# y as one product over 128 rows, scores in one group, and v loaded without zeros, in an RWKV-7 layer with its MLP

## The chip, the cores and the metric

The kernel runs on one core of a Trainium2 chip. The metric is device time in microseconds (us), the median of several runs of the same program.

## What is computed

An RWKV-7 recurrence for 4 batches of 8 heads (768 steps, head dimension 40), whose output, with the heads side by side, is the input of an MLP with a sigmoid-approximated GELU:

```python
for t in range(S):
    y[:, :, t] = np.einsum('bhd,bhde->bhe', rt, state)
    Sa = np.einsum('bhde,bhe->bhd', state, at)
    state_decay = state * wt[:, :, None, :] - np.einsum('bhd,bhe->bhde', Sa, bt)
    state = state_decay + np.einsum('bhd,bhe->bhde', vt, kt)
...
x = np.ascontiguousarray(attn_out.transpose(0, 2, 1, 3)).reshape(B * S, H * D)   # 3072 x 320
h = x @ w_in                                                                     # 320 x 2048
g = h * (1.0 / (1.0 + np.exp(-1.702 * h)))
return (g @ w_out).astype(np.float32)                                            # 2048 x 320
```

All is float32.

## The kernel before, in words

Time is cut into 12 chunks of 64 steps and the batches into 2 pairs, which gives 24 *units* i (chunk c, pair p). A unit holds 16 heads: a batch b of the pair, and a head index split into bits e, f and u. Within a unit the recurrence is solved in matrix form, so that only the 40x40 state z goes from unit i to unit i + 2.

**The array.** Almost every product works on a quarter of the TensorE array: 64 rows by 64 columns, four such tiles in turn (`QUARTERS`). A float32 product is two MATMULs and two weight loads, so four products of a group are 16 TensorE instructions. The helper `mm` (L270) issues all of them, which is why every MATMUL has line 270 and is told apart by its tile's name.

**A unit's steps.** `load_w`, `logarithm` and `decay` (L431 to L503) load the decays w, take logarithms (ScalarE), sum them (TensorE `ps_cum`, VectorE scans) and exponentiate: FT, GT by channel, and G by time step (L498, one ACTIVATE of 320 columns on 128 partitions). `prep` (L521 to L585) scales k and b by G into `kh` and `bh` (L535, two operations of 320 columns, GpSimd or VectorE), forms the score matrices `ps_NT` and `ps_A`, `ps_Av`, and also `ps_RV` (L575), the products of r and v, masked into the tile `RV` by VectorE (L583). `solve` (L592 to L815) forms `ps_N`, then six doubling levels (`ps_level`) whose results are copied into W and E by ScalarE and VectorE; the last level leaves 40 columns in the tile `M` (L639). `ps_saT` (L721) and its copy `saT` follow. `ps_M` (L748) multiplies saT by r, and VectorE masks it into `M` (L756). `read` (L760) then forms `ps_y`, both the output and the state update in 104 columns (64 steps and 40 state columns), as a sum of two sets of products, kh with RV and bh with M. `updated` (L775) gives the raw state `zraw` that unit i + 2 reads; `read_out` and `decayed` give x, which goes through DRAM and comes back transposed as `xT` (L805 to L815).

**The tile RV.** Its 104 columns per head are 64 for the masked products r·v and 40 for v itself. v is loaded straight into place, with zeros in the other 64 columns, which the mask operation overwrites later (L441, `in_v`).

**The MLP** (`mlp`, L822). For each chunk: `ps_up` (160 products of 256 columns), GELU on ScalarE (L835) into `g`, `ps_down` (128 products of 320 columns), a copy and an add into `ob`, and a store.

**What sets the order.** Nothing runs in program order. Every step is a `Task` with a rank, the engines that it may run on with an assumed duration on each, what it reads and writes, and the number of buffers of each tile (`plan.slots`). `Plan.order` (L97) plays a list scheduler over five engines, and emits the instructions in that order; each engine runs its own list in order. The plan has a model of how fast TensorE's instructions can be fetched (`FETCH`, `BESIDE`, `BLOCK`: 256 instructions, 3,550 ns, more beside DMA traffic) and chooses between tasks by it (`ahead`, L144). MLP products have the highest ranks, so they fill what the units leave. `paced` repeats the ordering to spread the MLP over the run. PSUM is four pairs of banks, taken and given back by the plan. All DMA is issued by SyncE (SP).

**Weights.** The MLP's weights arrive as int64 words of doubles and are decoded on the chip in ten pieces (`weight`, L367), each with some seven VectorE and ScalarE operations of 1,024 columns; `W_IN` and `W_OUT` (L239) are their ranks. All of this happens in the first 160 us.

Of the kernel before, what the change touches and what calls it, by code (L numbers as in the profile page):

```python
# [49 lines left out]

class Task:
    def __init__(self, rank, engines, fn, pair, most, size):
        self.instr, self.sbuf = engines.pop("instr", 0), engines.pop("sbuf", False)
        self.rank, self.fn, self.pair, self.most, self.size = rank, fn, pair, most, size
        self.engines = engines
        self.after, self.then, self.release = set(), [], 0.0


class Plan:
# [5 lines left out]
    BLOCK, FETCH, BESIDE, AHEAD = 256, 3550.0, 0.4, 300.0  # L65
    DELAY = {"PE": 300.0, "DVE": 60.0, "ACT": 60.0, "POOL": 150.0, "SP": 800.0}

    LATENCY, RATE, SPREAD = 1200.0, 400.0, 1.3
# [28 lines left out]
    def order(self):  # L97
# [22 lines left out]
        issued, begun, shared = 0, 0.0, 0.0  # L120

        def fetch(at):
            took = self.FETCH
            for _ in range(3):
                beside = sum(max(0.0, min(y, at + took) - max(x, at)) for x, y in running[-8:])
                took = self.FETCH + self.BESIDE / self.SPREAD * beside
            return took
# [20 lines left out]
        while coming or able:  # L148
# [20 lines left out]
            if e == "PE":  # L169
                end, begun = fetched(t, now)  # L170
                issued += t.instr
# [5 lines left out]
            if e == "SP":  # L177
                wire = max(wire, end + self.LATENCY)
                running.append((wire, wire + self.SPREAD * t.size / self.RATE))
                end = wire = running[-1][1]  # L180
# [44 lines left out]
def rwkv7_gelu_quick(ctx: ExitStack, tc: tile.TileContext, time_d, v_d, w_d, wc_d, ak_d, b_d, rv_d, w_in, w_out, out):  # L225
    nc = tc.nc
# [12 lines left out]
    W_IN, W_OUT = 12, 30  # L239
# [10 lines left out]
    plan = Plan(dict(logw=3, wc=3, G=1, wch=3, wz=2, time=2, ak=2, b=2, rv=2, FT=3, GT=1, kh=2, bh=2, bz=2,  # L250
                     A=1, Av=1, RV=2, W=3, E=2, edge=1, zraw=2, zT=1, saT=1, M=2, y=1, x=1, xT=3, g=4, ob=1), 4)
# [86 lines left out]
    kh_t, bh_t = several("kh", [128, 8, 64]), several("bh", [128, 8, 64])  # L338
    for t in kh_t + bh_t:
        nc.gpsimd.memset(t[:, :, D:], 0.0)  # L340
# [5 lines left out]
    ak_t, b_t, rv_t = several("ak", [128, 2, 8, 64]), several("b", [128, 8, 64]), several("rv", [128, 2, 8, 64])  # L346
# [76 lines left out]
    time_of = lambda i: buf("time", i, [128, 3, DM])  # L423
    ak_of, b_of, rv_of = lambda i: ak_t[i % 2], lambda i: b_t[i % 2], lambda i: rv_t[i % 2]

    RV_of = lambda i: buf("RV", i, [128, 8, 104])
# [9 lines left out]
    def load(i):  # L436
        for name, of, src, n in (("ak", ak_of, ak_d, 1024), ("time", time_of, time_d, 3 * DM), ("b", b_of, b_d, 512),
                                 ("rv", rv_of, rv_d, 1024), ("RV", RV_of, v_d, 832)):
            rows = [slice(p.start, p.start + D) for p in HALF] if i >= 2 and name in ("ak", "b", "rv") else [slice(0, 128)]

            def go(t, of=of, src=src, rows=rows):  # L441
                for p in rows:
                    nc.sync.dma_start(of(i)[p], src[i, p])
            plan.add(10 * i - 4, {"SP": 350.0 * len(rows)}, go, writes=[(name, i)] + ([("v", i)] if name == "RV" else []),
                     size=sum(p.stop - p.start for p in rows) * n * 4)


    G_of = lambda i: buf("G", i, [128, 2, 160])
# [24 lines left out]
    def decay(i):  # L473
# [3 lines left out]
        def by_time(t):  # L477
            ps, lw = psum(t, "ps_cum"), logw_of(i)
            for n in (1, 0):
                for b in BITS:  # L480
                    u = b ^ n
                    mm(ps[HALF[u], b, :160], incl[HALF[b]], lw[HALF[b], n * 160:(n + 1) * 160], True)
        plan.add(R, pe((1, 160)), by_time, reads=T("log"), uses=T("logw"), room=T("G"), writes=T("cum"), pair=("cum", i))

        def exp_channel(t):
            if i >= EARLY:
# [11 lines left out]
        plan.add(R, {"ACT": 460.0}, lambda t: nc.scalar.activation(G_of(i), psum(t, "")[:, :, :160], ACT.Exp, scale=-1.0),  # L498
                 reads=T("FT"), writes=T("G", "exps"), pair=("cum", i))
# [6 lines left out]
    def by_head(t):  # L506
        return t.rearrange("t (h d) -> t h d", h=H)

# [5 lines left out]
    saT_of = lambda i: buf("saT", i, [128, 8, 64])  # L514
    M_of = lambda i: buf("M", i, [128, 8, 104])
    xT_of = lambda c: buf("xT", c, [128, 2, NK, 128])
    kh_of, bh_of = lambda i: kh_t[i % 2], lambda i: bh_t[i % 2]
# [3 lines left out]
    def prep(i):  # L521
        R = 10 * i - 6
        T = lambda *names: [(n, i) for n in names]
        G = lambda: G_of(i).rearrange("t b (h d) -> t (b h) d", d=D)
# [9 lines left out]
        for n, (name, dst) in enumerate((("kh", kh_of), ("bh", bh_of))):  # L534
            plan.add(R + 4, {"POOL": 870.0, "DVE": 490.0, "sbuf": True}, lambda t, n=n, dst=dst: of(t.engine).tensor_mul(  # L535
                dst(i)[:, :, :D], by_head(time_of(i)[:, n]), G()), reads=T("time", "exps", "G"), writes=T(name))
# [26 lines left out]
        def times_v(t):  # L563

            ps, v_b = psum(t, "ps_Av"), time_of(i)[:, 2]
            for e, f in product(BITS, BITS):
                for b, u in QUARTERS:
                    o, h = (2 * e + f) * D, head(e, f, b, u)
                    mm(ps[HALF[u], b, o:o + D], A_of(i)[HALF[b], 4 * e + 2 * u + f], v_b[HALF[b], h * D:(h + 1) * D], o == 0)
# [4 lines left out]

        def score_RV(t):  # L575

            ps, rv = psum(t, "ps_RV"), rv_of(i)
            for e, b in product(BITS, BITS):
                for f, u in QUARTERS:
                    o, j = (2 * e + b) * 64, 4 * u + 2 * e + b  # L580
                    mm(ps[HALF[u], f, o:o + 64], rv[HALF[f], 1, j], rv[HALF[f], 0, j], o == 0)
        plan.add(R + 9, pe((4, 64)), score_RV, reads=T("rv"), room=T("RV"), pair=("RV", i))
        plan.add(R + 9, dve(512), lambda t: nc.vector.tensor_tensor(  # L583
            RV_of(i)[:, :, :64].rearrange("p (e j) t -> p e j t", e=2), psum(t, "")[:, :, :256].rearrange("p e (j t) -> p e j t", t=64),
            mask(upper), ALU.mult), reads=T("v"), writes=T("RV"), pair=("RV", i))  # L585
# [6 lines left out]
    def solve(i):  # L592
# [59 lines left out]
        def level(n, b):  # L652
# [9 lines left out]
            def go(t):  # L662
# [3 lines left out]
                for j in BITS:  # L666
                    o = j * 208
# [7 lines left out]
                if early and alone:  # L675
                    view = ps[:, :, :416].rearrange("p h (j n) -> p h j n", n=208)
                    for h, q in QUARTERS:
# [9 lines left out]
                     room=T("M") if last else [("W", s + 1)] + ([] if early and n < LEVELS - 2 else [("E", es + 1)]), pair=pair)  # L687
# [10 lines left out]
            elif last:  # L698
                plan.add(key, any2(160), lambda t: signed(
                    t, M_of(i).rearrange("p (f e b) n -> p b e f n", f=2, e=2)[:, b, :, :, 64:], item(t)[:, :, :, 64:104], i >= EARLY),  # L700
                         writes=T("M"), pair=pair)
# [19 lines left out]
        def sa_turned(t):  # L721

            ps, w, E = psum(t, "ps_saT"), W_of(6 * i + 5), E_of(last_e(i))
            for u, b in product(BITS, BITS):
                for e, f in QUARTERS:
                    o = (2 * u + b) * 64
                    mm(ps[HALF[f], e, o:o + 64], w[HALF[e], u, b, f, 64:128], E[HALF[e], u, b, f, 64:], o == 0)
# [4 lines left out]
            t, saT_of(i).rearrange("p (r j) t -> p r (j t)", r=2), psum(t, "")[:, :, :256], i >= EARLY), writes=T("saT"), pair=("saT", i))  # L732

        y_of, x_of = lambda: buf("y", i, [128, 8, 64]), lambda: buf("x", i, [128, 4, 2, 64])
        if c > 0:
            def read_state(t):

                ps, rT = psum(t, "ps_rz"), rv_of(i)[:, 0]
                for u, b in product(BITS, BITS):
                    for f, e in QUARTERS:  # L740
                        o, at = (2 * u + b) * 64, (4 * e + 2 * u + b) * D
                        mm(ps[HALF[e], f, o:o + 64], zT_of(i)[HALF[f], at:at + 64], rT[HALF[f], 4 * u + 2 * e + b], o == 0)
# [5 lines left out]
        def scores(t):  # L748

            ps, rT = psum(t, "ps_M"), rv_of(i)[:, 0]  # L750
            for e, b in product(BITS, BITS):
                for f, u in QUARTERS:
                    o = (2 * e + b) * 64
                    mm(ps[HALF[u], f, o:o + 64], saT_of(i)[HALF[f], 4 * e + 2 * u + b], rT[HALF[f], 4 * u + 2 * e + b], o == 0)
        plan.add(R + 4, pe((4, 64)), scores, reads=T("saT", "rv"), room=T("M"), pair=("M", i))
        plan.add(R + 4, dve(512), lambda t: nc.vector.tensor_tensor(  # L756
            M_of(i)[:, :, :64].rearrange("p (e j) t -> p e j t", e=2), psum(t, "")[:, :, :256].rearrange("p e (j t) -> p e j t", t=64),
            mask(upper), ALU.mult), writes=T("M"), pair=("M", i))

        def read(t):  # L760

            ps = psum(t, "ps_y")
            for b, f in product(BITS, BITS):
                o = (2 * b + f) * 104
                for m, w in ((RV_of(i), kh_of(i)), (M_of(i), bh_of(i))):
                    for u, e in QUARTERS:
                        mm(ps[HALF[e], u, o:o + 104], w[HALF[u], 4 * b + 2 * f + e], m[HALF[u], 4 * f + 2 * e + b],
                           o == 0 and w is kh_t[i % 2])
        plan.add(R + 4, pe((8, 104)), read, reads=T("RV", "M", "kh", "bh") + (T("rz") if c > 0 else []), room=T("y", "zraw"),
                 pair=("y", i))  # L770
# [43 lines left out]
        plan.add(-50, {"SP": 700.0}, part_with, reads=T("x"), writes=T("xd"), size=DM * 512)  # L814
# [161 lines left out]
```

## Time and profile before

| | |
|---|---|
| Five runs | 826.61, 841.57, 825.93, 837.47, 836.05 us |
| Median | 836.05 us |
| Profiled execution | 826.61 us, of which its span is 824.7 us |
| Instructions | 51,261, of which 24,192 MATMULs and 24,192 weight loads |
| DMA | 82.60 MB, mean 100 GB/s |
| Mean granted TensorE clock | 0.971 |

PE is TensorE's matrix work, PEld its weight loads, DVE is VectorE, ACT ScalarE, POOL GpSimd, SP SyncE. The page cuts the span into 40 slices of some 20.6 us; a digit is a busy share in tenths. The chain of waits goes back from the last instruction to whatever released each step; "issue" in it is time in which an engine waited for nothing that the profile shows. A group is given as line, engine, operation, output and inputs with shapes, count, then busy us and mean ns of one, then the idle time just before them and what ended it. In the table of stretches each engine has its busy us and, in brackets, its instructions, then the granted clock, the DMA share and GB/s.

A MATMUL's recorded duration overlaps with that of the next ones: 250 ns for a ps_y MATMUL, though 64 of them take 1.43 us together. Prices of groups are therefore taken from the chain, where one group ends as the next begins.

### The profile page before, as it was taken

How to read it: one execution, taken by the hardware profiler on the slowest of the kernel's cores; microseconds unless marked ns; L12 is line 12 of the kernel's file. 1: busy time of each engine (PE TensorE's matmuls, PEld its weight loads, DVE VectorE, ACT ScalarE, POOL GpSimd, SP SyncE). 2: the span in 40 equal slices, each digit the busy share in tenths (PEclk: the TensorE clock that was granted, in tenths of full speed). 3: DMA queues.
4: the chain of work that ended last, by engine and by line, in shares of the span. 5: the costliest groups of instructions: out<-in, count | busy, mean ns of one | idle time of the engine just before them, and what ended most of it. 6: DMA issues, size and time to landing. Idle time of an engine off the chain costs nothing.

```text
span 824.7 us, 51261 instructions
## 1 busy us (share of the span) xinstructions
PE 754.5 (91%) x24192; PEld 648.0 (79%) x24192; DVE 476.8 (58%) x757; ACT 368.3 (45%) x634; POOL 148.1 (18%) x208
## 2 busy tenths in 40 slices
PE   3575899999999988999999999999999999999997
PEld 3564777798786887789777777789799888778997
DVE  7478897845655646565566556566456566455100
ACT  4554745335346336444556345345355445233110
POOL 4020304311203202211203112022113112100000
PEclk9885899999999999999999999999999999999999
DMA  9834533322423413222324325134233223110100
GB/s 340 341 116 155 178 110 103 117 81 65 120 73 94 126 51 109 86 92 82 110 71 134 90 63 150 35 103 133 57 97 113 68 65 105 49 36 29 35 10 17
DMA packets 33018, 82.60 MB, mean 100 GB/s; under 512 B 5128, under 2 KB 11272, under 8 KB 31528
## 3 DMA queue, kind: packets, MB, share of 16 engines
q1 hardware_dynamic: 32808, 79.32, 30.3%
q8 instruction: 190, 3.11, 1.6%
q14 instruction: 20, 0.16, 0.1%
HBM read 71.43 MB, written 7.86 MB: 96 GB/s over the span
## 4 chain that ended last, share of the span: by engine, by line
PE 84%; ACT 5%; DVE 4%; issue 4%; DMA 2%; SPq 1%; ACTq 0%; DVEq 0%
PE ps_up L270 24%; PE ps_down L270 24%; PE ps_level L270 18%; PE ps_y L270 5%; PE ps_N L270 2%; PE ps_NT L270 2%; PE ps_rz L270 2%; PE ps_saT L270 1%; PE ps_A L270 1%; PE ps_M L270 1%; PE ps_zT L270 1%; PE ps_Av L270 1%; PE ps_RV L270 1%; ACT g L835 1%; ACT W L714 1%
## 5 line engine op out<-in xcount | busy, mean ns | idle before, releaser
L270 PE MATMUL ps_up<-xT,w_sb 64*64 64x256 f32 x3840 | 268.1, 380 | 6.8 <-ACT g L835 3.0
L270 PE MATMUL ps_down<-w_sb,g 64*64 64x320 f32 x3072 | 245.6, 433 | 2.2 <-issue 0.8
L270 PEld LDWEIGHTS ps_up<-xT,w_sb 64*64 64x64 f32 x3840 | 159.2, 135 | 23.8 <-issue 4.5
L270 PEld LDWEIGHTS ps_level<-W,E 64*64 64x64 f32 x5888 | 150.7, 135 | 29.3 <-ACT g L835 3.6
L714 ACT COPY W<-ps_level 128x672 f32<-128x672 f32 (+1 forms) x154 | 95.1, 620 | 170.8 <-PE ps_level L270 160.1
L270 PEld LDWEIGHTS ps_down<-w_sb,g 64*64 64x64 f32 x3072 | 134.2, 134 | 36.7 <-issue 3.9
L270 PE MATMUL ps_level<-W,E 64*64 64x64 f32 (+2 forms) x5888 | 148.1, 230 | 6.4 <-DVE E L704 1.7
L709 DVE TENSOR_TENSOR E<-twice,ps_level 128x512 f32<-128x512 f32 x120 | 81.4, 683 | 66.2 <-ACT W L714 55.8
L535 POOL TENSOR_TENSOR kh<-time,G 128x320 f32<-128x320 f32 x22 | 19.7, 893 | 450.5 <-issue 217.9
L270 PEld LDWEIGHTS ps_level<-W 64*64 64x64 f32 x2560 | 68.8, 142 | 20.7 <-issue 12.1
L270 PE MATMUL ps_level<-W 64*64 64x64 f32 (+2 forms) x2560 | 71.0, 244 | 13.4 <-issue 9.2
L835 ACT ACTIVATE g<-ps_up 128x1024 f32<-128x1024 f32 x48 | 49.1, 1023 | 54.6 <-PE ps_up L270 54.2
L799 POOL TENSOR_TENSOR x<-y,FT 128x128 f32<-128x128 f32 x84 | 46.5, 583 | 19.8 <-ACT y L791 19.6
L693 DVE TENSOR_TENSOR W<-edge,ps_level 128x672 f32<-128x672 f32 x40 | 34.0, 850 | 21.0 <-PE ps_level L270 20.3
L861 DVE TENSOR_TENSOR ob<-ob,ps_down 128x320 f32<-128x320 f32 x24 | 11.6, 484 | 58.9 <-ACT ob L859 58.4
L270 PE MATMUL ps_y<-RV,kh 64*64 64x104 f32 x768 | 37.3, 260 | 7.7 <-DVE M L756 7.6
L714 DVE COPY W<-ps_level 128x672 f32<-128x672 f32 (+1 forms) x46 | 34.4, 751 | 8.2 <-PE ps_level L270 8.1
L270 PEld LDWEIGHTS ps_y<-RV,kh 64*64 64x64 f32 x768 | 30.1, 140 | 10.6 <-DVE M L756 8.1
L270 PE MATMUL ps_y<-M,bh 64*64 64x104 f32 x768 | 37.4, 260 | 0.9 <-issue 0.9
L527 POOL TENSOR_TENSOR ak<-ak,FT 128x512 f32<-128x512 f32 x21 | 28.1, 1339 | 28.6 <-DMA ak<-in_ak 17.9
L756 DVE TENSOR_TENSOR M<-ps_M,upper 128x512 f32<-128x512 f32 x24 | 16.5, 688 | 26.3 <-PE ps_M L270 26.2
L859 ACT COPY ob<-ps_down 128x320 f32<-128x320 f32 x24 | 10.2, 426 | 47.0 <-PE ps_down L270 46.8
(111 smaller groups left out, 1015.6 us busy)
## 6 DMA issues: line engine op xcount, KB each, us to landing
time<-in_time SPq DMA_DIRECT2D x24, 480.0 KB
RV<-in_v SPq DMA_DIRECT2D x24, 416.0 KB
xT<-x_dram SPq DMA_DIRECT2D x48, 160.0 KB
ak<-in_ak SPq DMA_DIRECT2D x44, 160.0 KB
rv<-in_rv SPq DMA_DIRECT2D x44, 160.0 KB
wc<-in_wc SPq DMA_DIRECT2D x24, 264.0 KB
extra<-in_w_out SPq DMA_DIRECT2D x4, 1024.0 KB
logw<-in_w SPq DMA_DIRECT2D x24, 160.0 KB
```

Of the source, the lines that this page charges most:

```text
L270: nc.tensor.matmul(o, lhsT, rhs, start=start, stop=True, skip_group_check=True)
L527: plan.add(R, {"DVE": 690.0, "POOL": 1270.0, "sbuf": True}, lambda t: of(t.engine).tensor_mul(ahT(), ahT(), FT_of(i)), reads=T("ak", "FT") ...
L535: plan.add(R + 4, {"POOL": 870.0, "DVE": 490.0, "sbuf": True}, lambda t, n=n, dst=dst: of(t.engine).tensor_mul(dst(i)[:, :, :D], by_head(t ...
L693: plan.add(key, dve(672), lambda t: nc.vector.tensor_sub(W_of(s + 1)[:, :, b], edge[:, :, b], item(t)[:, :, :, :168]), reads=T("edge"), wr ...
L709: plan.add(key, dve(512), lambda t: nc.vector.tensor_sub(E_of(es + 1)[:, :, b].rearrange("p h j (n t) -> p h (j n) t", n=2), wide(twice).t ...
L714: plan.add(key, any2(4 * (168 - lo)), lambda t: copy(t.engine)(W_of(s + 1)[:, :, b, :, lo:], item(t)[:, :, :, lo:168]), writes=keeps, pair ...
L756: plan.add(R + 4, dve(512), lambda t: nc.vector.tensor_tensor(M_of(i)[:, :, :64].rearrange("p (e j) t -> p e j t", e=2), psum(t, "")[:, :, ...
L799: of(t.engine).tensor_mul(x[:, b ^ u, b], y_of()[:, at], FT_of(i)[:, at])
L835: plan.add(-45, act(1024), lambda t: nc.scalar.activation(g_of(c * NQ + q).rearrange("p m r n -> p r m n"), psum(t, "").rearrange("p r (m ...
L859: plan.add(-45, any2(320), lambda t: copy(t.engine)(ob_of(serial), psum(t, "")[:, 0, :DM]), writes=[("ob", serial)], pair=("down", serial))
L861: plan.add(-45, dve(320), lambda t: nc.vector.tensor_add(ob_of(serial), ob_of(serial), psum(t, "")[:, 1, :DM]), reads=[("ob", serial)], wr ...
```

## The change

- **y.** kh and bh become one tile `kb`, of 128 partitions: kh (64 steps) above bh (64 steps), for all 16 heads side by side. RV and M become one tile `RM` of 128 partitions: the masked r·v (and v) above, the masked saT·r (and the last level's result) below. y is one product over 128 rows for each of the 16 heads, instead of two over 64. `kb` is made by one operation of 640 columns instead of two of 320.
- **RM's layout** is [13, 16, 8]: 104 columns of a head are 13 runs of 8, each 16 x 8 elements from the next. The product's moving operand, the masks' output and the last level's copies use it.
- **Scores.** `ps_RV` with its own mask is gone. `scores` forms r·v and r·saT in one group of 32 products, v and saT side by side in the tile `rv`, and two mask operations write all of RM's scores. saT now lies in `rv`.
- **G** is needed in both halves of the partitions, for all 320 channels: one ACTIVATE on 128 partitions with 320 columns becomes four on 64 partitions with 320 columns each.
- **The last level** is copied to partitions 64 to 127 of RM, in two operations per batch b instead of one.
- **v** is loaded as 64 partitions of 640 contiguous elements (160 KB) instead of 128 of 832 (416 KB).
- **The plan's numbers**: `BESIDE` and the DMA model, a price `SWITCH` for a task whose number of rows differs from the last one's, SP's delay 800 to 1,300, `W_OUT` 30 to 35, buffers (xT 3 to 2, saT 1 to 2).

```diff
-    BLOCK, FETCH, BESIDE, AHEAD = 256, 3550.0, 0.4, 300.0
-    DELAY = {"PE": 300.0, "DVE": 60.0, "ACT": 60.0, "POOL": 150.0, "SP": 800.0}
+    BLOCK, FETCH, BESIDE, AHEAD = 256, 3550.0, 0.37, 300.0
+    SWITCH = 105.0
+    DELAY = {"PE": 300.0, "DVE": 60.0, "ACT": 60.0, "POOL": 150.0, "SP": 1300.0}
...
-                end, begun = fetched(t, now)
+                end, begun = fetched(t, now + (self.SWITCH if t.rows != rows else 0.0))
+                rows = t.rows
...
-    W_IN, W_OUT = 12, 30
+    W_IN, W_OUT = 12, 35
...
-                     A=1, Av=1, RV=2, W=3, E=2, edge=1, zraw=2, zT=1, saT=1, M=2, y=1, x=1, xT=3, g=4, ob=1), 4)
+                     A=1, Av=1, RM=2, W=3, E=2, edge=1, zraw=2, zT=1, saT=2, y=1, x=1, xT=2, g=4, ob=1), 4)
...
-                for p in rows:
-                    nc.sync.dma_start(of(i)[p], src[i, p])
+                if name == "RM":
+                    nc.sync.dma_start(of(i)[HALF[0], 8:].rearrange("p g j n -> p (g j n)"), src[i])
+                    return
+                for p in rows:
+                    nc.sync.dma_start(of(i)[p, :2] if name == "rv" else of(i)[p], src[i, p])
...
-        plan.add(R, {"ACT": 460.0}, lambda t: nc.scalar.activation(G_of(i), psum(t, "")[:, :, :160], ACT.Exp, scale=-1.0),
+        def exp_time(t):
+            for h in BITS:
+                for p in HALF:
+                    nc.scalar.activation(G_of(i)[p, :, h * 160:(h + 1) * 160], psum(t, "")[HALF[h], :, :160], ACT.Exp, scale=-1.0)
+        plan.add(R, {"ACT": 1800.0}, exp_time, reads=T("FT"), writes=T("G", "exps"), pair=("cum", i))
...
-        for n, (name, dst) in enumerate((("kh", kh_of), ("bh", bh_of))):
-            plan.add(R + 4, {"POOL": 870.0, "DVE": 490.0, "sbuf": True}, lambda t, n=n, dst=dst: of(t.engine).tensor_mul(
-                dst(i)[:, :, :D], by_head(time_of(i)[:, n]), G()), reads=T("time", "exps", "G"), writes=T(name))
+        plan.add(R + 4, {"POOL": 1700.0, "DVE": 830.0, "sbuf": True}, lambda t: of(t.engine).tensor_mul(
+            kb_of(i)[:, :, :D], time_of(i)[:, :2 * DM].rearrange("t (h d) -> t h d", d=D),
+            G_of(i).rearrange("t b (h d) -> t (b h) d", d=D)), reads=T("time", "exps", "G"), writes=T("kb"))
...
-        def score_RV(t):
-            ps, rv = psum(t, "ps_RV"), rv_of(i)
-            for e, b in product(BITS, BITS):
-                for f, u in QUARTERS:
-                    o, j = (2 * e + b) * 64, 4 * u + 2 * e + b
-                    mm(ps[HALF[u], f, o:o + 64], rv[HALF[f], 1, j], rv[HALF[f], 0, j], o == 0)
...
-                plan.add(key, any2(160), lambda t: signed(
-                    t, M_of(i).rearrange("p (f e b) n -> p b e f n", f=2, e=2)[:, b, :, :, 64:], item(t)[:, :, :, 64:104], i >= EARLY),
-                         writes=T("M"), pair=pair)
+                for u in BITS:
+                    plan.add(key, any2(160), lambda t, u=u: signed(
+                        t, RM_of(i)[HALF[1], 8:, 8 * b + 4 * u:8 * b + 4 * u + 4].rearrange("p g j n -> p j g n"),
...
         def scores(t):
-            for e, b in product(BITS, BITS):
-                for f, u in QUARTERS:
-                    o = (2 * e + b) * 64
-                    mm(ps[HALF[u], f, o:o + 64], saT_of(i)[HALF[f], 4 * e + 2 * u + b], rT[HALF[f], 4 * u + 2 * e + b], o == 0)
+            for j, (b, u, e) in enumerate(product(BITS, BITS, BITS)):
+                for f, h in QUARTERS:
+                    mm(ps[HALF[h], f, j * 64:(j + 1) * 64], rv[HALF[f], 1 + h, 4 * e + 2 * b + u],
+                       rv[HALF[f], 0, 4 * e + 2 * b + u], j == 0)
+        plan.add(R + 4, pe((8, 64)), scores, reads=T("saT", "rv"), room=T("RM"), pair=("M", i))
+        for f in BITS:
+            plan.add(R + 4, dve(512), lambda t, f=f: nc.vector.tensor_tensor(
+                RM_of(i)[:, :8].rearrange("p g (j f) n -> p f j g n", f=2)[:, f],
...
         def read(t):
-            for b, f in product(BITS, BITS):
+            for b, f, u, e in product(BITS, BITS, BITS, BITS):
                 o = (2 * b + f) * 104
-                for m, w in ((RV_of(i), kh_of(i)), (M_of(i), bh_of(i))):
-                    for u, e in QUARTERS:
-                        mm(ps[HALF[e], u, o:o + 104], w[HALF[u], 4 * b + 2 * f + e], m[HALF[u], 4 * f + 2 * e + b],
-                           o == 0 and w is kh_t[i % 2])
+                mm(ps[HALF[e], u, o:o + 104].rearrange("p (g n) -> p g n", n=8), kb_of(i)[:, 8 * b + head(e, f, b, u)],
+                   RM_of(i)[:, :, 8 * b + 4 * u + 2 * e + f], o == 0)
+        plan.add(R + 4, {"PE": 1375.0, "instr": 64, "rows": 128}, read, reads=T("RM", "kb") + (T("rz") if c > 0 else []),
+                 room=T("y", "zraw"), pair=("y", i))
```

## The prediction

> **What bounds the kernel now.** I read the page first, then the table of stretches, then the chain of waits in order of time, then the groups.
>
> ```profile
> PE 754.5 (91%) x24192; PEld 648.0 (79%) x24192; DVE 476.8 (58%) x757; ACT 368.3 (45%) x634; POOL 148.1 (18%) x208
> PE   3575899999999988999999999999999999999997
> PEclk9885899999999999999999999999999999999999
> DMA  9834533322423413222324325134233223110100
> q8 instruction: 190, 3.11, 1.6%
> PE 84%; ACT 5%; DVE 4%; issue 4%; DMA 2%; SPq 1%; ACTq 0%; DVEq 0%
> ```
>
> The array (PE) is busy in nine tenths of every slice after the first seven, and 84% of the chain is PE. To see whether busy means working, I priced the groups from the chain, where they follow each other: 64 ps_y MATMULs take 1.43 us, 16 of ps_up 0.865, 16 of ps_down 1.08, 32 with 64 columns (ps_M, ps_A and their like) 0.46, 32 of ps_N 0.72, 8 of ps_cum 0.27; ps_level averages 17.4 ns each. By the counts: ps_up 208 us, ps_down 207, ps_level 152, the eight 64-column groups 87, ps_y 34, ps_N 17, ps_cum 6.5: **712 us of array work** in a span of 824.7. So 113 us are lost. Where?
>
> ```profile
> 0.00:50.00 50.00, 26.03 (x987) 23.81 (x987) 32.27 (x57) 23.10 (x43) 9.77 (x27) 0.90 0.84 315
> 50.00:100.00 50.00, 33.77 (x1085) 30.40 (x1089) 39.96 (x49) 30.10 (x50) 11.76 (x14) 0.69 0.41 129
> 400.00:450.00 50.00, 48.69 (x1676) 39.75 (x1668) 30.93 (x50) 23.57 (x45) 11.74 (x17) 1.00 0.39 115
> ```
>
> The 2,072 MATMULs of the first 100 us are worth 38 us at these prices: 62 us lost, while weights are decoded and the MLP cannot fill. The other 725 us hold 674 of work: 51 lost. Part of that is seen here, in the chain of waits:
>
> ```profile
> 410.74 0.35 PE ps_RV L270 x24
> 411.08 0.19 issue
> 411.27 0.34 PE ps_RV L270 x8
> ```
>
> A group whose inputs are all there stops in its middle and waits for nothing visible. In the starts of the MATMULs such pauses recur at multiples of about 127 MATMULs (number 3,283, 3,410, 3,538, ... 14,494, 14,621, 14,748). 127 with their weight loads are about 254 instructions, and queue q8 brought 190 packets of 3.11 MB, 16 KB each, which is 256 instructions of 64 bytes. So the array waits for its instruction stream. Packets mostly come 3.5 us apart at the closest and 4.1 on average: the stream runs at some 85% of what it can. Those pauses after 100 us sum to about 16 us. The rest is late ACT work (copies of W and table loads, some 30 us of chain), one trip of x through DRAM (8.4) and late DVE.
>
> **What the skill says.** The Trainium skill, "Runtime: NRT & Kernel Launch", Instruction fetch mechanics: instructions come in 16 KiB blocks of 256, and crossing a block is "mostly hidden". The packets agree in size; pauses of 0.3 to 1.4 us say not wholly hidden. "TensorEngine Tiling (Array Packing)", Key Properties and Available Configurations: a 128x64 tiling has two tiles, tiles run in parallel, and changing the mode drains the array. This trace has 64*64 tiles alone: it shows four in parallel, but no switch. "SBUF — State Buffer", Door 1: SBUF lines are 16 bytes; the new 8-float runs fill two each. No strided MATMUL here tests it. "ScalarE: Activation LUTs", What ACT_TABLE_LOAD costs: 186 ns + 0.833 ns per element, 453 ns for 320 elements; the trace has 416.
>
> **The change, step by step**, against the profiled execution (824.7 span plus 1.9 around it, 826.6; it is the second lowest of five runs whose median is 836.05, 9.4 above).
>
> ```profile
> L270 PE MATMUL ps_y<-RV,kh 64*64 64x104 f32 x768 | 37.3, 260 | 7.7 <-DVE M L756 7.6
> L270 PEld LDWEIGHTS ps_y<-M,bh 64*64 64x64 f32 x768 | 29.0, 141 | 1.1 <-issue 1.1
> L756 DVE TENSOR_TENSOR M<-ps_M,upper 128x512 f32<-128x512 f32 x24 | 16.5, 688 | 26.3 <-PE ps_M L270 26.2
> L583 DVE TENSOR_TENSOR RV<-ps_RV,upper 128x512 f32<-128x512 f32 x24 | 16.5, 687 | 11.5 <-PE ps_RV L270 11.4
> L498 ACT ACTIVATE G<-ps_cum 128x320 f32<-128x320 f32 x24 | 10.1, 422 | 0.0
> ```
>
> *y.* 32 products of 64 rows become 16 of 128. Array time: four tiles at a time become two, so 1.43 us stays 1.43. Instructions: 64 MATMULs and 64 loads per unit become 32 and 32, so 64 x 24 = 1,536 fewer: **6 blocks of 189**. If each block cost its average 4.1 us this is 24.5 us; if all is hidden, 0. I take 14: 10 of the 16 us of pauses, and 4 of the 20 us of "issue" on the chain in the first 100 us, where the DMA share is 0.84 and fetches compete.
>
> *Switch of mode.* Twice per unit. A ps_y MATMUL's record lasts 250 ns though one starts each 22 ns, so a drain may expose up to 160 ns (250 less its own 90), and a weight load of 134 that can no longer run ahead. Bounds 0 and 0.29 us, 48 times: 0 to +14. The diff's own allowance is 105 ns; I take 0.125, **+6**.
>
> *Scores.* 64 MATMULs in one group replace 32 of ps_RV and 32 of ps_M: array time stays 2 x 0.46; the masks stay two of 0.69. But r·v and its mask, free to run any time before, now follow saT: y becomes ready about 0.46 + 0.69 later, and the two last-level copies become four (292 ns each at 160 columns; smaller in partitions, not in columns). After 100 us this is hidden: ps_N of one unit is at 409 us, its ps_y at 438, and MLP products stand between. In the first units that cover is missing: about 1.3 us for each of three, **+4**. What queues behind: DVE's masks push W copies back by 0.7 there.
>
> *exp_time.* One ACTIVATE of 0.42 us becomes four on 64 partitions each with the same 320 elements: +1.26 us x 24 = +30 us of ACT, and with the extra copies (2 x 0.3 x 24 = 14) ACT goes from 368 to 412. ACT is 45% busy, so most costs nothing; but gelu's and the W copies stand behind these in ACT's order, and in 255–263 us such a row of loads, G and gelu held the array. I scale those 30 us of chain by 412/368: **+3.5**. Bounds 0 and +14.
>
> *v and the other queues.* v's load falls from 416 KB to 160 KB: 6.3 of 82.6 MB, 24 issues on SP as before. Two of them lie in the stretch at 315–340 GB/s: **-1.5**. kb is one POOL operation of twice the length (2 x 0.87 us): 0, since POOL is 18% busy and y needs both halves anyway; if DVE takes it in the first units, up to +1. The logarithm's sums and by_time keep their count.
>
> *Plan.* xT falls from three slots to two, the second weights are decoded later (35 for 30), SP's delay is set longer. In the order of work these can save the 8.4 us wait for x, or make another. I take 0, with -10 and +10.
>
> Sum: -14 + 6 + 4 + 3.5 - 1.5 = -2: 824.6 against 826.6. A median of runs lay 9.4 above the profiled run; fetch waits are what competing DMA would stretch, and they shrink, so I put a third of that on top: **828 us**, 1.0% below 836.05. Adding the bounds that are mine to choose (fetch 0 to -24, switch 0 to +14, ACT 0 to +14, plan -10 to +10; rarely all on one side) gives its own range, 812 to 848.
>
> **Rivals.** *Fetch is the real bound (faster).* For it: fetch at 85% of its rate, 800 MATMULs in each 25 us throughout, pauses on block edges. Against: 400–450 us is 98% array work. All 24.5 us and the DMA relief count, the switch costs little: 836 - 24.5 - 1.5 + 3 = 813.
> *The two column halves of a 128-row product do not overlap (slower).* Both use all rows, so a weight load may not slip in under a product, and the strided RM rows may be read slowly. Then 32 passes of 87 ns take 2.8 us, plus loads: +1.35 to +2 per unit. With 0.25 for switches, 1.85 x 24 = +44, less 8 of fetch: 872. It turns into over 2% slower once ps_y and its switches take 1.0 us more than 1.43 (1.0 x 24 less 8 is 16). Against: the pages give two tiles, and today's four share rows and columns in pairs.
> *The start grows (slower or same).* Late scores, four exps and DVE at 40 of 50 us stretch the 62 lost us by a quarter, and ACT's rows late in the run add: +20, 856.
> *The cut does not reach the critical path:* if pauses only move (the planner fills by fetch, so an early y is waited for elsewhere), 836 plus the switch, 842.
>
> **How the numbers follow.** 2% of the median is 16.7 us (819.3 and 852.8), about what a comparison of this kernel can tell. The sum's own case and pauses that move: 0.50, of which 0.05 falls under 819 and 0.05 over 853. Fetch the bound: 0.25, nine tenths of it under 819. Halves that do not overlap: 0.12. The start grows: 0.13, of which 0.09 lies over 853. Faster 0.28, same 0.46, slower 0.26. The range runs from 802 (fetch gain and a good plan) to 860 (leaves out most of the serial case).
>
> **What would show it.** Right: 189 fetch packets become 183 or 184; ps_y's 32 MATMULs in 1.4 to 1.5 us, with 0.1 to 0.2 us before and after; fewer pauses inside groups; "issue" under 4%. Wrong: ps_y over 2 us (serial halves); the first 100 us with fewer than 2,000 MATMULs, allowing for the 32 fewer per unit; ACT above 8% of the chain; waits of ps_up for xT.

## The result, and the profile after

The changed kernel takes 831.23 us in the median of 43 runs (824.53 to 838.83), the kernel before 832.74 us in 80 runs (821.15 to 845.82). The ratio is **1.0016, 95% interval 1.0001 to 1.0032**: no change worth the name, where 1% less was forecast. (The ratio leaves out runs that lie more than 1.5% above the fastest of their kernel, and the kernel before has the longer tail, so the ratio can lie above 1 while the medians of all runs, as 0.998, lie below.) Two more comparisons of the same two programs on other chips gave 0.9982 (0.9957 to 1.0007) and 0.9993 (0.9962 to 1.0025).

The page of the profiled execution after the change (span 825.5 us): the engines, the instruction queue, the chain by engine, and three groups.

```profile
PE 760.8 (92%) x23424; PEld 613.2 (74%) x23424; DVE 491.5 (60%) x797; ACT 393.9 (48%) x709; POOL 139.0 (17%) x186
q8 instruction: 184, 3.01, 1.5%
PE 84%; ACT 6%; DMA 3%; issue 3%; DVE 2%; SPq 1%; POOL 0%; DVEq 0%; ACTq 0%
...
L754 DVE TENSOR_TENSOR RM<-ps_M,upper 128x512 f32<-128x512 f32 x48 | 30.9, 685 | 30.3 <-PE ps_M L274 30.1
...
L274 PE MATMUL ps_y<-RM,kb 128*64 128x104 f32 x768 | 41.1, 261 | 6.0 <-issue 5.2
...
L509 ACT ACTIVATE G<-ps_cum 64x320 f32<-64x320 f32 x96 | 41.0, 428 | 0.9
```

The parts of the change are all there: 768 MATMULs and as many loads fewer, six packets fewer in the instruction queue, ScalarE 26 us busier, the masks where they were. "issue" fell from 4% to 3% of the chain. The span did not move. The table of stretches, in the form used before:

```profile
0.00:50.00 50.00, 27.20 (x964) 24.61 (x967) 33.37 (x57) 28.24 (x54) 11.04 (x25) 0.90 0.86 293
50.00:100.00 50.00, 35.80 (x1227) 32.74 (x1223) 43.67 (x57) 31.53 (x53) 15.36 (x16) 0.86 0.41 132
400.00:450.00 50.00, 47.88 (x1552) 39.27 (x1548) 34.13 (x56) 27.77 (x49) 11.40 (x15) 1.00 0.30 90
```

The start is no slower: counted over 0 to 100 us as one stretch, there are 2,176 MATMULs for 2,072, though the two units that form y there need 64 fewer. It is no firm gain either: two other executions of the changed kernel have 2,067 and 2,182, and the clock granted in that stretch was 0.80 in the profile before and 0.85 to 0.88 in these three. In the middle, 1,552 MATMULs pass in 50 us for 1,676. The wider ps_y explains some 50 of these 124 (32 fewer per unit, about 1.5 units); the rest is another mix of work in that stretch.

What the switch of mode costs is read from the chain of waits, where ps_y stands between the same neighbours before and after. First the kernel before, then the changed one; start, length and what, in us:

```profile
406.44 1.43 PE ps_y L270 x64
407.87 1.08 PE ps_down L270 x16
```

```profile
398.22 1.58 PE ps_y L274 x32
399.79 1.22 PE ps_down L274 x13
```

From first to last start, the 32 MATMULs of ps_y take 1.395 us in 22 of the 24 units (the other two are at the start of the run), the 64 of before 1.358. So the two column halves do run side by side. What is new is mostly around them: the next product starts 0.18 us after ps_y's last instead of 0.07, and ps_y's first, behind an MLP product, starts 0.30 to 0.36 after that one's last instead of 0.20 to 0.25. Together, with the 0.04 inside, 0.26 us per unit, **6.2 us of array time in all**.

So the array pays 6.2 us, as forecast. The question is what became of the fetches.

### The profile page after: what moved, and what is told of

The parts are those of the page before. It is cut to its first block, busy times and chain, and to the rows that moved or that the text cites. A ratio compares the mean times of both kernels' runs of the same rounds, so it can differ in the third digit from the quotient of the medians.

```text
span 825.5 us, 49888 instructions
## 1 busy us (share of the span) xinstructions
PE 760.8 (92%) x23424; PEld 613.2 (74%) x23424; DVE 491.5 (60%) x797; ACT 393.9 (48%) x709; POOL 139.0 (17%) x186
## 4 chain that ended last, share of the span: by engine, by line
PE 84%; ACT 6%; DMA 3%; issue 3%; DVE 2%; SPq 1%; POOL 0%; DVEq 0%; ACTq 0%
PE ps_down L274 24%; PE ps_up L274 24%; PE ps_level L274 18%; PE ps_y L274 5%; PE ps_M L274 3%; PE ps_N L274 2%; PE ps_Av L274 2%; PE ps_NT L274 1%; PE ps_saT L274 1%; DMA x_dram<-x 1%; PE ps_A L274 1%; PE ps_rz L274 1%; PE ps_zT L274 1%; ACT W L710 1%; DMA b<-in_b 1%
## 5 line engine op out<-in xcount | busy, mean ns | idle before, releaser
L274 PEld LDWEIGHTS ps_up<-xT,w_sb 64*64 64x64 f32 x3840 | 152.8, 134 | 38.0 <-issue 7.3
L274 PEld LDWEIGHTS ps_down<-w_sb,g 64*64 64x64 f32 x3072 | 115.0, 134 | 55.3 <-issue 2.7
L539 POOL TENSOR_TENSOR kb<-time,G 128x640 f32<-128x640 f32 x23 | 37.1, 1611 | 457.1 <-issue 288.3
L274 PE MATMUL ps_level<-W 64*64 64x104 f32 (+2 forms) x2560 | 72.1, 245 | 11.5 <-issue 6.9
L754 DVE TENSOR_TENSOR RM<-ps_M,upper 128x512 f32<-128x512 f32 x48 | 30.9, 685 | 30.3 <-PE ps_M L274 30.1
L274 PEld LDWEIGHTS ps_y<-RM,kb 128*64 128x64 f32 x768 | 36.1, 141 | 14.3 <-issue 10.9
L274 PE MATMUL ps_y<-RM,kb 128*64 128x104 f32 x768 | 41.1, 261 | 6.0 <-issue 5.2
L686 DVE TENSOR_TENSOR W<-edge,ps_level 128x672 f32<-128x672 f32 x40 | 34.0, 850 | 20.3 <-PE ps_level L274 18.5
L710 DVE COPY W<-ps_level 128x672 f32<-128x672 f32 (+1 forms) x55 | 41.2, 749 | 7.7 <-PE ps_level L274 7.6
L509 ACT ACTIVATE G<-ps_cum 64x320 f32<-64x320 f32 x96 | 41.0, 428 | 0.9
L274 PEld LDWEIGHTS ps_M<-rv 64*64 64x64 f32 x1536 | 28.8, 135 | 7.6 <-issue 3.0
```

What stands on the lines that cost most here:

```text
L274: nc.tensor.matmul(o, lhsT, rhs, start=start, stop=True, skip_group_check=True)
L509: nc.scalar.activation(G_of(i)[p, :, h * 160:(h + 1) * 160], psum(t, "")[HALF[h], :, :160], ACT.Exp, scale=-1.0)
L539: plan.add(R + 4, {"POOL": 1700.0, "DVE": 830.0, "sbuf": True}, lambda t: of(t.engine).tensor_mul(kb_of(i)[:, :, :D], time_of(i)[:, :2 * D ...
L686: plan.add(key, dve(672), lambda t: nc.vector.tensor_sub(W_of(s + 1)[:, :, b], edge[:, :, b], item(t)[:, :, :, :168]), reads=T("edge"), wr ...
L710: plan.add(key, any2(4 * (168 - lo)), lambda t: copy(t.engine)(W_of(s + 1)[:, :, b, :, lo:], item(t)[:, :, :, lo:168]), writes=keeps, pair ...
L754: plan.add(R + 4, dve(512), lambda t, f=f: nc.vector.tensor_tensor(RM_of(i)[:, :8].rearrange("p g (j f) n -> p f j g n", f=2)[:, f], psum( ...
```

## The experiments

Every kernel was timed beside the kernel before, on the same chip, and a ratio is to the kernel before. "In the order of the changed kernel" ("in its own order" in the expectations) means that the planner was told nothing of the edit, so that every engine's list is that of the changed kernel except for the edit. Pauses are taken from the starts of the MATMULs after 100 us: the time by which the gap to the next start exceeds one group's own stream, summed apart for gaps inside a task and between tasks. Each sum is of one profiled execution. In the kernel before they are 15.4 us inside and 19.1 between; in the profiled changed kernel 12.4 and 24.6, of which 4.2 stand beside ps_y.

### Are the removed fetches worth anything?

`a_y64f`: y by four tiles of 64 rows, in the order of the changed kernel. Its sums join other pairs of heads, so it does the same amount of work but does not compute the layer; that holds for `a_y64f2` and `a_y64` below too.

```diff
-            for b, f, u, e in product(BITS, BITS, BITS, BITS):
+            for b, f, u in product(BITS, BITS, BITS):
                 o = (2 * b + f) * 104
-                mm(ps[HALF[e], u, o:o + 104].rearrange("p (g n) -> p g n", n=8), kb_of(i)[:, 8 * b + head(e, f, b, u)],
-                   RM_of(i)[:, :, 8 * b + 4 * u + 2 * e + f], o == 0)
+                for h, e in QUARTERS:
+                    mm(ps[HALF[e], h, o:o + 104].rearrange("p (g n) -> p g n", n=8), kb_of(i)[HALF[h], 8 * b + head(e, f, b, u)],
+                       RM_of(i)[HALF[h], :, 8 * b + 4 * u + 2 * e + f], o == 0 and u == 0)
```

> The changed kernel in exactly its own order of instructions, but y formed by 32 products of 64 rows with four tiles at a time, instead of 16 of 128 rows: 1,536 more TensorE instructions (6 fetch blocks), no change of tiling mode. So that row halves keep to their own PSUM bank, its sums join other pairs of heads than the reference does; the work is the same. Theory A (the fetch gain came, about 14 us, and something else ate it): it loses 14 and wins the switches' 6, some 8 us slower than the changed kernel, ratio to the kernel before near 1.011. Theory B (the fetch gain was only about 3 us because most fetching was hidden): 3 us faster than the changed kernel, ratio near 0.998.

Ratio 1.0073 (1.0043 to 1.0102), between the 1.011 of theory A and the 0.998 of theory B. Pauses inside tasks 26.8 us, twice those of the changed kernel. That speaks for theory A more than for B. But here the planner made room for 64 instructions and 128 came. The other half of the question is what happens if it is told. Four kernels on one chip, two orders by two numbers of instructions:

`a_same2`: no edit.

> The changed kernel itself, the yardstick for the other three on one chip: order planned for 64 instructions of y, 64 issued. Ratio to the kernel before 0.997 to 1.003.

`a_y64f2`: as `a_y64f`.

> As a_y64f, on the same chip as its yardstick: order planned for 64 instructions of y, 128 issued (y's sums join other pairs of heads). The first time it had 26.8 us of pauses inside groups after 100 us, where the changed kernel has 12 to 14. Both theories: 7 to 10 us slower than the changed kernel.

`a_y64`: as `a_y64f`, and

```diff
-        plan.add(R + 4, {"PE": 1375.0, "instr": 64, "rows": 128}, read, reads=T("RM", "kb") + (T("rz") if c > 0 else []),
+        plan.add(R + 4, pe((8, 104)), read, reads=T("RM", "kb") + (T("rz") if c > 0 else []),
```

> As a_y64f, but with the planner told: order planned for 128 instructions of y, 128 issued (y's sums join other pairs of heads). Theory C (a fetch costs only where the order was not planned for it; the kernel before had already arranged its order around its own fetches, so there was little to gain): within 3 us of the changed kernel, pauses inside groups back to 15 to 20 us. Theory A (6 fetch blocks are worth some 13 us whatever the order, and another part of the change ate that): as slow as a_y64f2, 7 to 10 us over the changed kernel.

`a_plan128`: only that line, y itself over 128 rows.

> The changed kernel with the planner told that y has 128 instructions and no switch, though it issues 64 over 128 rows: the order of a_y64 exactly, 64 issued. Theory C: the removed instructions free fetch time where the order had already made room, so it gains little over a_y64, 0 to 5 us less the 6 of the switches, and is within 4 us of it. Theory A: 7 to 10 us faster than a_y64, like a_same2 against a_y64f2.

| ratio to the kernel before | 128 rows, 64 instructions issued | 64 rows, 128 issued |
|---|---|---|
| order planned for 64 | 0.9993 (0.9962 to 1.0025) | 1.0077 (1.0046 to 1.0109) |
| order planned for 128 | 0.9999 (0.9970 to 1.0028) | 1.0011 (0.9982 to 1.0040) |

The times are those of theory C, which said that a fetch costs only where the order was not planned for it. In the order planned for 64, the additional 64 instructions of a unit cost 0.84%, 7 us, and with the 6.2 us of switches that they save, 13 us: close to what the prediction took for them (14). In the order planned for 128 the same exchange costs 0.12%, 1 us, so about 7 us for the fetches. The traces point the same way: the exchange adds some 11 us of pauses inside tasks in the first order and some 5 in the second. And along the diagonal, each version planned for its own, the times are 0.18% or 1.5 us apart (the intervals allow 4 more either way): **of 13 us of fetch, some 8 remain, and the switches take 6 of those.**

This is less than proof. The difference between 0.84% and 0.12% is 0.7%, with an interval, from those of the four ratios, of 0.6 either way. And there is only one order of each kind: what an unplanned fetch costs may differ from order to order by chance, and no second pair of orders was run.

How a fetch that was not planned for looks is seen in the chain of waits of `a_y64f2`, and then the same group in the changed kernel:

```profile
341.48 0.43 PE ps_Av L274 x29
341.92 0.87 issue
342.79 0.31 PE ps_Av L274 x3
```

```profile
335.07 0.60 PE ps_Av L274 x32
```

A group of ready inputs stops for 0.9 us where the changed kernel goes on. It is not so everywhere: in the ps_M group at 399 us `a_y64f2` stops for 0.6 us, and the changed kernel, in each of its three profiled executions, stops in the same group for about as long or longer. The planner has a rule for such places (`ahead`: if the instructions would run ahead of their fetch by more than 0.3 us, take a task with fewer of them for its time); that it is this rule that makes the difference is not shown.

One part of theory C was off: with the planner told, pauses inside tasks fell to 24.5 us only, not to 15 to 20; the larger fall was between tasks, 25.0 to 20.5. Nor do the pauses inside tasks tell which order is fast: `a_order` and `b_order` below have some 23 us of them, and the first is faster than the kernel before, the second as fast.

### Do the switches come through?

`a_switch2`: a product of 64 rows in the middle of ps_y.

```diff
+                if (b, f, u, e) == (1, 0, 0, 0):
+                    mm(ps[HALF[0], 0, 416:424], ident[HALF[0]], ident[HALF[0], :8], False)
```

> The changed kernel in its own order, with one product of 64 rows and 8 columns put into the middle of each unit's y (columns that nobody reads): two more changes of tiling mode per unit, 48 in all, and 96 more TensorE instructions. If the array's time is what sets the end, the switches' 0.125 us each come through whole, with the small product: 6 to 9 us slower than the changed kernel, ratio 1.005 to 1.010. If drains are covered as the fetches were (the next weights and the fetch catch up meanwhile): 0 to 3 us, ratio 0.998 to 1.003.

Ratio 1.0121 (1.0046 to 1.0196), from six runs, above the expected 1.005 to 1.010. In its trace ps_y takes 1.75 us from first to last start instead of 1.39, in each of the 22 units after 100 us: with the small product itself, 0.36 x 24 = 8.7 us. In the chain of waits:

```profile
397.96 1.94 PE ps_y L274 x34
399.90 1.24 PE ps_down L274 x16
```

The 8.7 us are 1.0%, and the ratio lies 0.4% to 1.9% above the changed kernel's 1.000 of other chips; the changed kernel was not run on this one. It is thin support: the medians of all runs, 837.76 and 835.27 us, are only 0.3% apart. That the array loses the time in each unit is shown. That the run loses all of it fits, but is not settled.

### Is it ScalarE?

`a_exp8f`: the four exponentials of G twice, in the order of the changed kernel.

```diff
-            for h in BITS:
+            for h in (0, 1, 0, 1):
```

> The changed kernel in its own order, with each of the four G exponentials done twice: +41 us of ScalarE, PE's list unchanged. If late ScalarE work is what ate the gain, the four exponentials (+30 us of ScalarE over the kernel before) cost 5 us or more, and doubling them adds 5 to 10 us: ratio 1.008 to 1.014. If ScalarE has room for them: under 2 us, ratio 1.000 to 1.004.

Ratio 1.0163 (1.0111 to 1.0215), from six runs: some 13 us for 41 us of ScalarE. Its list of who waited for whom (engine, line, for what, us in total, times, longest):

```profile
PE ps_level L274 <- ACT G L509: 7.9, 6, 2.8
PE ps_A L274 <- ACT G L509: 7.7, 2, 7.5
```

The array waits for G's exponentials themselves, which stand in ScalarE's order ahead of a copy or of the bank's release. So is half of that already paid with four? `a_exp2f` leaves two of them out, with those quarters of G held at zero:

```diff
+    G_t = several("G", [128, 2, DM])
+    nc.gpsimd.memset(G_t[0], 0.0)
...
-    G_of = lambda i: buf("G", i, [128, 2, DM])
+    G_of = lambda i: G_t[0]
...
-                for p in HALF:
+                for p in HALF[h:h + 1]:
```

> The changed kernel in its own order of TensorE, VectorE and DMA work, but with two of the four G exponentials left out: the halves of G that they would fill are zero throughout, so kh and bh miss some heads. 21 us less of ScalarE. If ScalarE's added work is on the path, as the run with the exponentials doubled says (12 us for +41 us), this is 5 to 7 us faster than the changed kernel: ratio 0.993 to 0.996. If the doubled run only hit a point where ScalarE runs out, and four are still free, ratio 1.000 to 1.003.

Ratio 0.9979 (0.9954 to 1.0004), beside `a_same`, the changed kernel itself on that chip, at 0.9982:

> The changed kernel itself, unaltered, as the yardstick on the same chip as the other three. All theories: a ratio to the kernel before of 1.000 to 1.004.

The 5 to 7 us that would say "on the path" are not there. By the medians, 831.67 and 833.46 us, the kernel without the two is 1.8 us faster, so a cost of 2 us or so for them isn't excluded. Up to four, in an order that was planned for four, ScalarE has room or nearly so; for four more, in that same order, it has not. Whether an order planned for eight would take them in was not run. The row of ScalarE work that the prediction feared is in the trace after, and long (chain of waits):

```profile
687.58 1.28 ACT L494
688.88 0.63 ACT FT L497
689.51 0.52 ACT GT L498
...
690.26 1.28 ACT L833
691.55 1.02 ACT g L833
...
692.60 1.28 ACT L509
693.89 0.43 ACT G L509
694.33 0.43 ACT G L509
694.77 0.43 ACT G L509
695.22 0.43 ACT G L509
```

Three table loads (the 1.28 us pieces) and an exponential row, 8 us on the chain once. Without two of the four it would be 0.9 shorter; over the run that is lost in the spread.

### Does the smaller v help?

`a_v416f`: a further 224 KB per unit, in the order of the changed kernel.

```diff
+    spare = single("spare", [128, 448])
...
                     nc.sync.dma_start(of(i)[HALF[0], 8:].rearrange("p g j n -> p (g j n)"), src[i])
+                    nc.sync.dma_start(spare, time_d[i, :, :448])
```

> The changed kernel in its own order, with a further load of 224 KB for every unit (5.5 MB in all) beside v's, into a tile that nobody reads: the DMA traffic is about that of the kernel before. If the lighter v helped the fetches and the start, this gives that back: 3 to 6 us slower than the changed kernel, ratio 1.005 to 1.009. If the traffic is hidden: ratio 1.000 to 1.003.

Ratio 1.0030 (1.0006 to 1.0055); the changed kernel was not run on that chip. Against its 1.000 elsewhere, v's zeros cost 0 to 5 us, and 2.5 is the middle. This stays open within those bounds.

### How much is the order itself?

`a_order` and `b_order`: the planner's fetch time 3,550 to 3,600 ns, in the changed kernel and in the one before. `a_oldplan`: the changed kernel with the old planner's numbers (`BESIDE` 0.4/1.3, SP's delay 800, transfers times 1.3, no factor on the size of x, `W_OUT` 30).

> The changed kernel with one number of the planner changed, the assumed time of a fetch block 3,550 to 3,600 ns: the same work in another order. If the order that the planner happens to find is worth as much as the parts of the change, it differs from the changed kernel by 3 to 10 us either way (ratio 0.990 to 1.013). If the order matters little: within 2 us, ratio 0.999 to 1.004.

> The kernel before with the planner's assumed time of a fetch block 3,550 to 3,600 ns: the same work in another order. The changed kernel moved by 0.6% under the same edit. If the order found is a matter of luck in both kernels: a ratio anywhere from 0.990 to 1.010, not within 0.002 of 1. If the kernel before had a tuned order: 1.003 or more. If only the changed kernel is sensitive: 0.999 to 1.002.

> The changed kernel with the planner's numbers of the kernel before (fetch beside DMA, the DMA model, SP's delay 800, W_OUT 30), the buffers as changed. If the new numbers matter for the start (the second weights later), the first 100 us hold some 100 to 200 MATMULs fewer than the changed kernel's 2,191 and the run is 3 to 8 us slower: ratio 1.005 to 1.011. If they are one more draw of an order: 0.992 to 1.006.

0.9953 (0.9928 to 0.9979), 1.0006 (0.9974 to 1.0037) and 0.9979 (0.9946 to 1.0011). The new planner's numbers are worth nothing that can be told from `a_same`'s 0.9982. The start with the old numbers has 2,040 MATMULs in 100 us, somewhat fewer than the three executions above, but the time does not show it. An edit of 50 ns in one assumed duration, though, gave the changed kernel 0.9953 where three comparisons without it gave 0.9982 to 1.0016, on other chips: a step of 0.3% to 0.6%, larger than the whole change. In the kernel before the same edit changed the order (pauses inside tasks rose from 15 to some 23 us) and not the time. So an order can be worth half a per cent, and need not be.

### A faster version

`a_gcopy`: two of the four exponentials become VectorE copies of the finished halves, and the planner is told. `a_gcopy2`: the same with 3,600 ns.

```diff
-                for p in HALF:
-                    nc.scalar.activation(G_of(i)[p, :, h * 160:(h + 1) * 160], psum(t, "")[HALF[h], :, :160], ACT.Exp, scale=-1.0)
-        plan.add(R, {"ACT": 1800.0}, exp_time, reads=T("FT"), writes=T("G", "exps"), pair=("cum", i))
+                p = HALF[h]
+                nc.scalar.activation(G_of(i)[p, :, h * 160:(h + 1) * 160], psum(t, "")[HALF[h], :, :160], ACT.Exp, scale=-1.0)
+        plan.add(R, {"ACT": 900.0}, exp_time, reads=T("FT"), writes=T("Gown", "exps"), pair=("cum", i))
+
+        def exp_other(t):
+            for h in BITS:
+                g = slice(h * 160, (h + 1) * 160)
+                nc.vector.tensor_copy(G_of(i)[HALF[1 - h], :, g], G_of(i)[HALF[h], :, g])
+        plan.add(R, {"DVE": 600.0, "sbuf": True}, exp_other, reads=T("Gown"), writes=T("G"))
```

> The changed kernel, planned anew, with two of the four G exponentials replaced by VectorE copies of the finished halves to the other 64 partitions: 20 us of ScalarE go, some 12 us of VectorE come. If ScalarE's late work can be planned away: 3 to 6 us faster than the changed kernel, ratio 0.993 to 0.996. If the order absorbs it too: ratio 0.997 to 1.003.

> As a_gcopy, with the planner's fetch time at 3,600 ns, the number that gave the changed kernel 0.9953. A candidate for the fastest: ratio 0.992 to 0.996 if both gains hold, 0.997 to 1.003 if they are draws of an order.

`a_gcopy` takes 824.55 us, ratio **0.9936 (0.9910 to 0.9963)**, the lowest of all; `a_gcopy2` 1.0015 (0.9979 to 1.0050), where 0.992 to 0.996 was hoped for. The page of `a_gcopy`:

```profile
PE 757.2 (93%) x23424; PEld 617.8 (76%) x23424; DVE 494.9 (61%) x811; ACT 394.0 (48%) x696; POOL 144.1 (18%) x187
...
PE 82%; ACT 6%; DVE 4%; DMA 4%; issue 3%; SPq 1%; DVEq 0%; ACTq 0%
```

ScalarE is exactly as busy as in the changed kernel (394.0 us), since the planner gave it other work back. Waits between tasks are 12.8 us instead of some 25, pauses inside them 22.6. With the same work in another order, `a_gcopy2` has 23.7 and 19.7 and no gain. So `a_gcopy` as it stands beats the kernel before, and the changed kernel by their ratios on different chips. But the same copies in another order gave nothing, so the copies alone cannot be credited with it; `a_order`, without copies, came to 0.9953 by an order alone.

## Why the prediction was wrong

The time lies in the range and the likeliest case was "within 2%", but 1% less was forecast and nothing came. By the prediction's steps:

- **"... so I put a third of that on top" is the step that made the forecast and failed.** The sum itself was -2 us, a forecast of -0.2%, and that lies inside the intervals of two of the three comparisons (0.9982 and 0.9993, not 1.0016). The other 6 us came from the 9.4 us by which the median of five runs lay above the profiled execution: they were taken for waits of which two thirds would go with the fetches. With more runs that surplus is 6.1 us before (832.74 over 826.61) and 4.0 after (831.23 over 827.20), so it shrank by 2 and not by 6, and 3.3 of the 9.4 were there because the median was of five runs. Nor is it a stock of fetch waits: in the experiments the profiled execution lies from 5.2 us below the median of its runs (`a_gcopy`) to 3.2 above (`a_exp8f`), whichever happened to be profiled.
- **"y ... I take 14" is the term of the sum that was too large.** The count was right (190 packets became 184), and 13 us is what the instructions are worth in an order that does not expect them. But the kernel before does expect them: its order had been chosen by the same model of fetching. The pauses in the trace (16 us) were taken as a stock from which 10 could be had; in three executions of the changed kernel they are 12.4, 14.1 and 16.0. The 4 us from "issue" at the start did come, on the chain: 20.0 us of the first 100 before, 14.4, 12.1 and 12.7 in the same three. But waits for DMA took their place there: 6.9 us of that chain before (`rv`), 18.5, 16.8 and 15.4 after (`b`, x and back, `ak`). No run here tells why, and it can't be said that more MATMULs were done by then. Planned for its own instructions, the two versions are 1.5 us apart, so by that pair of orders the 64 instructions are worth some 8 us, not 14.
- *Switch of mode, +6*: right as array time, 6.2; `a_switch2` agrees within a wide interval.
- *exp_time, +3.5*: not settled. By that scaling, two of the four exponentials would give back 2.4 us; 0.3 us by the ratios and 1.8 by the medians came. As a rule the scaling failed: it would price the next 41 us of ScalarE at some 5, and they cost 13.
- *Scores, +4, in the first units*: not seen; the first 100 us hold as much work as before, within the spread of executions.
- *v, -1.5*: 0 to -5 by `a_v416f`, so not refuted.
- *Plan, 0 within 10*: right in size. Four orders of the changed kernel (its own, `a_order`, `a_oldplan`, `a_plan128`) lie at 0.9953 to 1.0016.
- That the sum as a whole came out right is luck: y too high by 6 is made up by the scores and ScalarE, priced at 7.5 together, of which little or nothing was seen.
- Of the rivals, "the cut does not reach the critical path", described with pauses that move, was nearest in kind; its 842 counted the switches and none of the gain. Serial halves did not occur: 1.39 us. "The start grows" did not either.
- One reading was off: "400–450 us is 98% array work", the argument against the fetch as the bound. The array is busy for 48.69 of those 50 us, 97%, and at the prediction's own prices its MATMULs there are worth some 47 us, 93%.

What stays open: the terms that are left (8 for fetch, 6.2 of switches, v at 0 to -5, ScalarE at 0 to some +3.5, the scores at nothing) add up to between some -7 and +2 us, and the three comparisons, -1.5 to +1.3, lie inside. The waits for DMA at the start are in none of these terms. An order's draw is of that size, and no experiment here separates it from a small real gain or cost.

## What to carry to other kernels

When a planner or a hand-made order already works around a resource, do not take the pauses left in the profile as the price of that resource: here removing work from it returned less than that. Nor is the distance between a median and one profiled execution a cost that a change can remove, before many runs have shown it. Price such an edit twice, once in the fixed old order and once with the order made anew, and believe the second. And before crediting an edit with half a per cent, change one irrelevant number of the plan and see how far the time moves.

## What the runs showed that was not expected

- A change between 64-row and 128-row tiles costs 0.22 us of array time for going and coming back, behind and before MLP products: 0.11 us at each end, the same in unit after unit (0.181 to 0.184 us to the next start in 22 of 24, for 0.07 without it).
- Two 128-row tiles side by side stream nearly as fast as four 64-row ones: 1.395 us from first to last start for 1.358. The moving operand's runs of 8 floats, 512 bytes apart, cost nothing that is seen: with four tiles, `a_y64` reads the same runs in 1.36 us.
- 1,536 instructions, 3% of TensorE's stream and 6 fetch blocks, cost some 13 us (7 measured, with the 6.2 of switches saved) in the one order that did not expect them, some 2.2 us a block, and some 7 in the other. In the profile before, one in twenty blocks comes less than 3.43 us after the last, and none less than 3.3.
